# Two engine assignments for the splitting of weights in the first MoE: odd lo parts on VectorE, every third low word on ScalarE

## The chip, the cores and the metric

The kernel runs on one core of one Trainium2 chip. The time is device microseconds of one execution. Three runs of the kernel before took 1201.35 to 1202.64 us, with a median of 1201.83.

## The reference, cut to what matters

Attention over 4 batches of 12 heads (448 tokens, 64 per head, with RMS norm of q and k) is followed by two MoE blocks without a gate. All weights arrive as float64.

```python
scores = scale * q_n @ k_n.T
attn = exp(scores - max) / sum
x = (attn @ v).transpose(0, 2, 1, 3).reshape(1792, 768)
h = x @ w_in                    # 768 x 2048
x2 = (relu(h) ** 2) @ w_out     # 2048 x 768
y = ((x2 @ w1) * (x2 @ w2)) @ w3 @ moe2_w_out
```

## The kernel before, in words

**Three products for one.** TensorE multiplies float32 operands as fp32r, with fewer bits. So each operand is kept as two parts: hi, the value copied into fp32r, and lo, the value less hi. `mm3` (its matmuls are lines 403, 404 and 405) adds up hi x hi, hi x lo and lo x hi. A part of a weight is a stationary 128x128 block, the activations of one batch (448 tokens) move.

**From float64 to two parts.** A weight unit is a block of 128 x 384 or 128 x 512 weights. On its first use it comes from HBM as pairs of 32-bit words, into one of four `raw64` buffers (`load_next`, the DMA on line 313, SyncE's queue). `words` makes the high word into the top bits of a float32 on ScalarE (line 327) and the low word's top 16 bits into its lowest bits, either on ScalarE (line 331) or on GpSimd (line 333); which of them is read from `LOW_ENG`. `join` shifts and ors the two on VectorE (line 340) into a float32 tile in a `raw` buffer, and so frees the `raw64` buffer. `store` writes that tile to a scratch tensor (`f_in`, `f_out`, `f_1`, `f_2`) on SyncE's queue (line 348), from where later batches load it as float32. `split_hi` copies it into the hi part on ScalarE (line 138, by `copy_on`). `split_lo` subtracts hi from it into the lo part, on VectorE or GpSimd (line 145, by `sub_on`); which of them is read from `LO_ENG`. The lo part is the last reader of the `raw` buffer.

**Units.** `units` lists them in order of use. Numbers 0 to 31 belong to the product w3 x w_out of the second MoE, which is made first. Numbers 32 to 119 are the float64 units of the first batch's MoE: 32 of w_in (384 wide), 24 of w_out (512 wide), 32 of w1 and w2 (384 wide), in the order 16 of w_in, 12 of w_out, 16 of w_in, 12 of w_out, 32 of w1 and w2. All later ones are float32. `U0` is 32 and `U1` is 120, so `LOW_ENG[1]` and `LO_ENG[1]` are read for 32 to 119 alone; from 120 on the lo part has a rule of its own.

**Order of the work.** The loop over 48 heads at the end of the kernel mixes each head's attention with a generator of matmuls (`fill`): w3 x w_out beside batch 0's heads, the first batch's MoE (`gen_moe(0)`) beside batch 1's heads, and so on. `advance(u)` keeps the loads five units, the words three, the joins two and the hi parts one unit ahead of the lo parts, and the lo parts four ahead of the unit in use. The order in which an engine issues is not the emitted one: a planner of the framework chooses it from its own costs of the instructions. Only from the third batch on SyncE's queue is held to the emitted order, and every engine in the tail (`in_order`, `chain`).

**Attention on the same engines.** For a head, TensorE makes scores `sc` (lines 925 and 926), VectorE their maxima `nb` (927), ScalarE the exponents `p` (949), TensorE turns them into `pt` (985), ScalarE copies that into the hi part of `ptr` (138), VectorE makes its lo part (145) and TensorE multiplies by v into `kv` (1026). In the second batch p goes through a DMA `pw<-p` on the way (955). `ql` (897) is a part of the next head's q on VectorE; `act` is the activation inside the MoE (474 to 479), whose lo part is on VectorE for the first batch; `x` is the attention's output, whose lo part is on GpSimd.

The two tables of engines, and the lines that read them:

```python
LOW_ENG = ("gga", "g")                 # 65
LO_ENG = ("ggggv", "ggv")              # 66
low_eng = LOW_ENG[i >= U0]             # words, 329
if low_eng[i % len(low_eng)] == "a":   # 330
lo_eng = LO_ENG[i >= U0]               # split_lo, 368
eng = lo_eng[i % len(lo_eng)] if i < U1 else "g"
```

Of the kernel before, what the change touches and what calls it, by code (L numbers as in the profile page):

```python
# [30 lines left out]
def attention_moe_kernel(  # L31
# [30 lines left out]

    LOW_ENG = ("gga", "g")
    LO_ENG = ("ggggv", "ggv")
    KHI_ENG = "ggvv"
    KLO_ENG = "gvvv"
    QHI_ENG = "avvv"
# [254 lines left out]
    def words(i):  # L324
# [3 lines left out]
        low = t.rearrange("p n t -> p (n t)").bitcast(U16).rearrange("p (n t) -> p n t", t=4)[:, :n, 1]  # L328
        low_eng = LOW_ENG[i >= U0]
        if low_eng[i % len(low_eng)] == "a":  # L330
# [34 lines left out]
    def split_lo(i):  # L365
        n = units[i][0].shape[-1]
        t = hls[i]
        lo_eng = LO_ENG[i >= U0]
        if i >= u_at["pair"]:
# [837 lines left out]
```

## Time and profile before

| | us |
|---|---|
| median of three runs | 1201.83 (1201.35 to 1202.64) |
| the profiled execution | 1196.79 |
| its span, first to last instruction | 1195.0 |
| share of TensorE's full clock, mean over the span | 0.978 |

The profile is of one execution. PE is TensorE's matrix unit, PEld its weight load, DVE is VectorE, ACT is ScalarE, POOL is GpSimd, SPq is SyncE's queue of DMAs. A row of the table by stretch has the stretch, its length, then for PE, PEld, DVE, ACT and POOL the busy us with the number of instructions, the granted clock as a share of full speed, the DMA engines' share and GB/s. A row of a group has the line, the engine, the operation, out<-in by the program's names, shapes and count; then the busy us and the mean ns of one; then the engine's idle time just before the group's instructions and what ended it. A row of waits has who waited for whom, the us in total, how often and the longest. A row of one line has the shortest, the middle and the longest duration in ns. A row of the timeline has the start in us, the duration in us, the instruction, and in brackets its engine's idle time before it with what ended that. A matmul's duration overlaps with the next one's.

### The profile page before, as it was taken

To read this page: it belongs to the slowest core of one execution; us is meant where nothing else is said; L and a number is where in the kernel's file an instruction comes from. 1 tells how busy PE (TensorE), PEld (TensorE's weight loads), DVE (VectorE), ACT (ScalarE), POOL (GpSimd) and SP (SyncE) were. 2 spreads that over 40 slices of the span, in tenths; PEclk is the share of its full clock that TensorE was granted. 3 is DMA by queue.
4 is the path that set the end of the run, shared out by engine and by line. 5 is a ranking of instruction groups with operands and counts; after the bars stand their busy time and mean duration, and the time that the engine had idled before them with its cause. 6 is when DMAs were issued, how large, how long until landed. Compare 5 with 4: busy or idle time off the path is not lost.

```text
span 1195.0 us, 19065 instructions
## 1 busy us (share of the span) xinstructions
PE 1148.4 (96%) x6054; PEld 1033.2 (86%) x6054; DVE 783.7 (66%) x1311; ACT 781.8 (65%) x1802; POOL 721.7 (60%) x708
## 2 busy tenths in 40 slices
PE   7799999998998999999999999999999999999998
PEld 4588788887897879998989999998999999799997
DVE  6689888877877854665565565564543213887786
ACT  6799878767767766767766677676773535433352
POOL 6776535555676766766785767485774858421131
PEclk8699999999998999999999999999999999999999
DMA  7777757788877884566664657665555656343433
GB/s 233 225 222 214 224 152 224 263 260 270 261 262 256 271 257 150 173 176 185 185 204 145 197 168 246 194 204 155 176 156 178 186 167 187 96 130 108 124 89 118
DMA packets 127811, 229.74 MB, mean 192 GB/s; under 512 B 15744, under 2 KB 80480, under 8 KB 127712
## 3 DMA queue, kind: packets, MB, share of 16 engines
q1 hardware_dynamic: 125984, 225.79, 61.9%
q10 hardware_dynamic: 1728, 2.75, 0.6%
q8 instruction: 47, 0.77, 0.3%
q14 instruction: 52, 0.43, 0.1%
HBM read 162.53 MB, written 37.05 MB: 167 GB/s over the span
## 4 chain that ended last, share of the span: by engine, by line
PE 53%; DMA 4%; ACT 4%; DVE 3%; issue 2%; POOL 2%; SPq 0%; ACTq 0%; POOLq 0%; DVEq 0%
PE mm L403 13%; PE mm L404 13%; PE mm L405 13%; PE kv L1026 3%; PE pt L985 2%; DMA raw<-w 1%; PE sc L926 1%; PE sc L925 1%; ACT p L949 1%; PE pt L404 1%; PE pt L405 1%; PE sc L404 1%; PE sc L405 1%; PE sc L403 1%; PE pt L403 1%
## 5 line engine op out<-in xcount | busy, mean ns | idle before, releaser
L145 POOL TENSOR_TENSOR hl<-raw,hl 128x384 fp32r<-128x384 f32 (+1 forms) x317 | 379.3, 1204 | 228.6 <-ACT hl L138 180.1
L138 ACT ACTIVATE hl<-raw 128x384 fp32r<-128x384 f32 (+1 forms) x405 | 226.5, 565 | 158.0 <-PE mm L405 32.4
L404 PE MATMUL mm<-x,hl 128*128 128x448 f32 (+1 forms) x640 | 237.5, 371 | 7.9 <-POOL x L145 7.9
L403 PE MATMUL mm<-x,hl 128*128 128x448 f32 (+1 forms) x640 | 240.5, 376 | 0.6 <-ACT x L138 0.6
L405 PE MATMUL mm<-x,hl 128*128 128x448 f32 (+1 forms) x640 | 236.3, 369 | 0.0
L404 PE MATMUL mm<-act,hl 128*128 128x448 f32 (+1 forms) x544 | 200.9, 369 | 5.1 <-POOL act L145 3.6
L403 PE MATMUL mm<-act,hl 128*128 128x448 f32 (+1 forms) x544 | 203.3, 374 | 0.8 <-ACT act L477 0.8
L405 PE MATMUL mm<-act,hl 128*128 128x448 f32 (+1 forms) x544 | 199.3, 367 | 0.0
L927 DVE TENSOR_REDUCE nb<-sc 112x1 f32<-112x448 f32 x192 | 115.3, 617 | 86.9 <-PE sc L926 85.7
L949 ACT ACTIVATE p<-sc,nb,rr 112x448 f32<-112x448 f32 x192 | 138.2, 722 | 5.8 <-DVE nb L929 3.4
L404 PEld LDWEIGHTS mm<-x,hl 128*128 128x128 f32 x640 | 122.9, 192 | 19.0 <-POOL x L145 9.8
L403 PEld LDWEIGHTS mm<-x,hl 128*128 128x128 f32 x640 | 122.8, 192 | 10.5 <-ACT x L138 1.0
L405 PEld LDWEIGHTS mm<-x,hl 128*128 128x128 f32 x640 | 123.0, 192 | 9.8
L333 POOL TENSOR_SCALAR raw<-raw 128x384 uint32<-128x384 uint16 (+1 forms) x110 | 77.4, 704 | 76.4 <-DMA raw<-w_in 31.5
L340 DVE SCALAR_TENSOR_TENSOR raw<-raw 128x384 uint32<-128x384 uint32 (+1 forms) x120 | 95.1, 800 | 43.3 <-POOL raw L333 24.5
L145 DVE TENSOR_TENSOR ptr<-pt,ptr 128x448 fp32r<-128x448 f32 x144 | 86.2, 617 | 52.4 <-ACT ptr L138 52.2
L404 PEld LDWEIGHTS mm<-act,hl 128*128 128x128 f32 x544 | 103.5, 190 | 15.5 <-POOL act L145 6.3
L403 PEld LDWEIGHTS mm<-act,hl 128*128 128x128 f32 x544 | 103.8, 191 | 8.8 <-ACT act L477 1.2
L405 PEld LDWEIGHTS mm<-act,hl 128*128 128x128 f32 x544 | 103.6, 190 | 7.8
L478 DVE TENSOR_TENSOR gf<-mm,r 128x448 f32<-128x448 f32 x64 | 39.6, 620 | 80.6 <-ACT r L474 76.0
L327 ACT ACTIVATE raw<-raw 128x384 f32<-128x384 f32 (+1 forms) x120 | 70.4, 595 | 29.2 <-DMA raw<-w_in 14.5
L145 POOL TENSOR_TENSOR act<-gf,act 128x448 fp32r<-128x448 f32 x64 | 77.0, 1204 | 13.3 <-DMA pw<-p 4.9
(149 smaller groups left out, 2188.7 us busy)
## 6 DMA issues: line engine op xcount, KB each, us to landing
pw<-p SPq DMA_DIRECT2D x72, 392.0 KB
raw<-f_in SPq DMA_DIRECT2D x96, 192.0 KB
raw<-f_out SPq DMA_DIRECT2D x72, 256.0 KB
raw<-w_in SPq DMA_DIRECT2D x32, 384.0 KB
raw<-w_out SPq DMA_DIRECT2D x24, 512.0 KB
raw<-w SPq DMA_DIRECT2D x32, 384.0 KB
qt<-q_t SPq DMA_DIRECT2D x48, 224.0 KB
raw<-f SPq DMA_DIRECT2D x56, 192.0 KB
```

Source lines behind the costliest of these rows:

```text
L138: nc.scalar.activation(out=out, in_=in_, func=AF.Copy)
L145: (nc.vector if eng == "v" else nc.gpsimd).tensor_tensor(out=out, in0=in0, in1=in1, op=op)
L327: nc.scalar.activation(out=hi, in_=hi, func=AF.Prelu, scale=2.0**-112, alpha=-(2.0**32))
L333: nc.gpsimd.tensor_scalar(out=t[:, :n, 0], in0=low, scalar1=2.0**-13, scalar2=2.0**-14 - 0.5, op0=ALU.mult, op1=ALU.add)
L340: nc.vector.scalar_tensor_tensor(out=f[:, :n].bitcast(U32), in0=t[:, :n, 1], scalar=3, in1=t[:, :n, 0], op0=ALU.logical_shift_left, op1=AL ...
L403: nc.tensor.matmul(ps, w[:, 0, wk, :], x[0], start=(i == 0), stop=False)
L404: nc.tensor.matmul(ps, w[:, 0, wk, :], x[1], start=False, stop=False)
L405: nc.tensor.matmul(ps, w[:, 1, wk, :], x[0], start=False, stop=(i == last))
L478: nc.vector.tensor_tensor(out=gf, in0=ps, in1=r, op=ALU.mult)
L927: nc.vector.tensor_reduce(out=nb[:, j:j + 1], in_=o[j], axis=AX.X, op=ALU.max, negate=True)
L949: nc.scalar.activation(out=p, in_=o[j], func=AF.Exp, scale=d["rq"][:, c:c + 1], bias=nb[:, j:j + 1], accum_out=sm[:, i, c:c + 1],)
L1026: nc.tensor.matmul(ps[:, :S], w, m, start=(n == 0), stop=(n == len(ops) - 1))
```

## The change

```diff
-    LOW_ENG = ("gga", "g")
-    LO_ENG = ("ggggv", "ggv")
+    LOW_ENG = ("gga", "gga")
+    LO_ENG = ("ggggv", "gv")
```

Of units 32 to 119, those whose number leaves 2 when divided by 3 (30 units: 22 of 384 and 8 of 512) have their low word made on ScalarE, where all 88 were on GpSimd. The lo part is made on VectorE for the odd numbers (44 units: 32 of 384 and 12 of 512), where it was for those that leave 2 when divided by 3 (30 units: 22 and 8); the others are on GpSimd. What is computed, the buffers and the transfers stay.

## Rows read from the trace of the kernel before

**Rows 1.** The page, part 1: busy us, share of the span, instructions.

```profile
PE 1148.4 (96%) x6054; PEld 1033.2 (86%) x6054; DVE 783.7 (66%) x1311; ACT 781.8 (65%) x1802; POOL 721.7 (60%) x708
```

**Rows 2.** The table by stretch, for the first MoE and what follows.

```profile
99.00:434.00 335.00, 313.24 (x1698) 279.32 (x1697) 276.36 (x474) 255.08 (x611) 201.71 (x219) 0.98 0.77 242
...
434.00:1195.00 761.00, 752.24 (x3955) 688.82 (x3953) 435.64 (x703) 449.85 (x1026) 451.73 (x410) 0.99 0.55 166
```

**Rows 3.** Waits of PE, 99 to 434 us.

```profile
PE sc L925 <- ACT p L949: 6.4, 10, 1.8
PE pt L985 <- DVE ptr L145: 6.2, 7, 2.7
PE pt L985 <- DMA pw<-p: 3.3, 2, 2.2
PE mm L404 <- DVE act L145: 1.5, 1, 1.5
PE kv L1026 <- DVE ptr L145: 1.4, 1, 1.4
PE mm L404 <- POOL x L145: 1.3, 2, 0.8
```

**Rows 4.** The table by stretch, of a piece at half clock.

```profile
361.40:368.10 6.70, 6.08 (x21) 5.18 (x22) 6.21 (x13) 3.65 (x11) 5.28 (x7) 0.50 0.99 347
```

**Rows 5.** Groups of POOL by shape, 99 to 434 us: low words and lo parts.

```profile
L145 POOL TENSOR_TENSOR hl<-raw,hl 128x384 fp32r<-128x384 f32 x42 | 48.1, 1148 | 17.1 <-ACT hl L138 14.9 <-PE kv L1026 0.8
L333 POOL TENSOR_SCALAR raw<-raw 128x384 uint32<-128x384 uint16 x64 | 41.0, 640 | 53.5 <-DMA raw<-w_in 31.5 <-DMA raw<-w 11.5 <-DVE vhl L142 4.0
L145 POOL TENSOR_TENSOR hl<-raw,hl 128x512 fp32r<-128x512 f32 x22 | 31.5, 1435 | 6.2 <-ACT hl L138 5.5
L333 POOL TENSOR_SCALAR raw<-raw 128x512 uint32<-128x512 uint16 x24 | 20.3, 846 | 15.9 <-DMA raw<-w_out 10.9 <-DVE nb L927 1.7 <-PE sc L926 1.4
```

**Rows 6.** Groups of ACT by shape, 0 to 120 us: low words.

```profile
L331 ACT ACTIVATE raw<-raw 128x512 uint32<-128x512 uint16 x5 | 3.4, 671 | 0.0
...
L331 ACT ACTIVATE raw<-raw 128x384 uint32<-128x384 uint16 x5 | 2.8, 550 | 0.0
```

**Rows 7.** Timeline of ACT, two evictions and the next one.

```profile
145.84 0.96 ACT L138 ACTIVATE ptr<-pt 128x448 fp32r<-128x448 f32 x2
146.69 0.54 ACT L138 ACTIVATE kt<-kv 128x448 fp32r<-128x448 f32 x1
```

**Rows 8.** Groups of DVE by shape, 99 to 434 us: joins and lo parts.

```profile
L340 DVE SCALAR_TENSOR_TENSOR raw<-raw 128x384 uint32<-128x384 uint32 x64 | 49.6, 783 | 32.2 <-POOL raw L333 15.7 <-ACT raw L327 6.3 <-POOL hl L145 4.3
...
L340 DVE SCALAR_TENSOR_TENSOR raw<-raw 128x512 uint32<-128x512 uint32 x27 | 24.8, 929 | 3.8 <-POOL raw L333 3.0 <-DMA raw<-w_out 0.5 <-issue 0.3
L145 DVE TENSOR_TENSOR hl<-raw,hl 128x384 fp32r<-128x384 f32 x22 | 15.6, 708 | 1.8 <-ACT hl L138 1.7
...
L145 DVE TENSOR_TENSOR hl<-raw,hl 128x512 fp32r<-128x512 f32 x9 | 7.4, 819 | 0.0
```

**Rows 9.** Line 340 on DVE, 99 to 434 us: durations, idle before it.

```profile
L340 DVE SCALAR_TENSOR_TENSOR raw<-raw x91: 543/678/2369, 101.8 to 426.5; 128x384 uint32<-128x384 uint32 x64, 128x512 uint32<-128x512 uint32 x27
...
  POOL raw L333: 18.7, 12
  ACT raw L327: 6.3, 4
  POOL hl L145: 4.3, 4
```

**Rows 10.** Line 145 on DVE, 99 to 434 us: durations of weights' lo parts.

```profile
L145 DVE TENSOR_TENSOR hl<-raw,hl x31: 543/675/1374, 123.9 to 432.9; 128x384 fp32r<-128x384 f32 x22, 128x512 fp32r<-128x512 f32 x9
```

**Rows 11.** Timeline around 320 us: POOL, DVE and the matmul behind them.

```profile
319.93 1.29 POOL L145 TENSOR_TENSOR hl<-raw,hl 128x512 fp32r<-128x512 f32 x1 [0.95 <-ACT hl L138]
...
320.54 1.17 DVE L897 SCALAR_TENSOR_TENSOR ql<-qt,gg,qh 128x448 fp32r<-128x448 f32 x1
...
322.30 0.47 PE L404 MATMUL mm<-act,hl 128*128 128x448 f32 x1 [1.47 <-DVE act L145]
```

## The prediction

> **What bounds the kernel now.** The page comes first. It says that TensorE's matrix unit was busy 1148.4 of 1195.0 us, 96%, while VectorE, ScalarE and GpSimd stood at 66%, 65% and 60% [rows 1]: only TensorE's 46.6 idle us, and what it lost at half clock, can be won back by moving work between the other three. The second view is the table by stretch, for the change touches 88 weight units that are handled between 99 and 434 us and nothing else. In that stretch TensorE is busy 313.2 of 335.0 us, so it is idle 21.8 us, and its mean granted clock is 0.98 [rows 2]. Behind 434 us it is idle only 761.0 - 752.2 = 8.8 us: what is gained or lost in the stretch is handed to the end almost whole, and nothing behind it can be gained by this change.
>
> The same table gives the three helpers there: VectorE 276.4 us (82%), ScalarE 255.1 (76%), GpSimd 201.7 (60%) [rows 2]. The change takes work from the idlest and gives it to the two busiest.
>
> The third view is who TensorE waited for in that stretch [rows 3]. The reader should see two things. No matmul waits for a weight (hl): every row is attention or activation work. And by engine the waits are ScalarE 6.4 us (the exponents p), VectorE 6.2 + 1.5 + 1.4 = 9.1, a DMA 3.3, GpSimd 1.3. GpSimd, which the change relieves, is directly behind 1.3 us of 21.8. The weights matter only through the queues: an instruction of theirs stands in front of an exponent or of a part of p.
>
> The clock belongs to the price of a stall. Of the stretch's time 2% of full clock is missing, that is 0.02 x 335 / 0.5 = 13.4 us at the lower level, 1.2 GHz. One such piece, 361.4 to 368.1, is at 0.50 [rows 4]; the engine was busy 6.08 of its 6.7 us, and work done there takes twice as long, so it cost some 3.4 us, and one of half its length would cost 1.7. All that could come back in the stretch is thus 21.8 + 6.7 = 28.5 us.
>
> **The change part by part.** The units are numbered 32 to 119: 64 of 128x384 words and 24 of 128x512.
>
> *Low words.* Every third unit (number mod 3 = 2) is 22 narrow and 8 wide ones. GpSimd loses 22 x 0.640 + 8 x 0.846 = 20.8 us [rows 5]. ScalarE gets the same ones in the form it already runs on the first 32 units: 22 x 0.550 + 8 x 0.671 = 17.5 us [rows 6]. Neighbours on ScalarE overlap: two evictions take 0.96 us together, and the next one starts at 146.69, before they end at 146.80 [rows 7]. Less 0.11 us each, the queue grows by 17.5 - 3.3 = 14.2 us, and ScalarE's idle time falls from 79.9 to 65.7 us.
>
> *Lo parts.* Before, 30 units (mod 3 = 2) go to VectorE; after, the 44 odd ones. 29 move to VectorE and 15 move back, so the net is 14: 10 narrow, 4 wide. GpSimd loses 10 x 1.148 + 4 x 1.435 = 17.2 us [rows 5]; VectorE gains 10 x 0.708 + 4 x 0.819 = 10.4 us [rows 8]. GpSimd goes to 201.7 - 20.8 - 17.2 = 163.7 us, 49% of the stretch.
>
> *What VectorE gets back.* Its instructions that read two operands from SBUF are stretched. The narrow join takes 0.783 us on average and 0.543 at best, the narrow lo part 0.708 and 0.543 [rows 8 to 10]. That is 64 x 0.240 + 22 x 0.165 = 19.0 us; the wide joins at the same share of their 24.8 us add 7.6. With 38.0 / 201.7 = 19% less GpSimd work I take 19% of 26.6 us: 5.0 us. The bounds are nothing, if the pairs that meet stay the same, and all 26.6.
>
> How GpSimd stretches VectorE is to be seen at 320 us: a GpSimd lo part runs from 319.93 to 321.22, VectorE's ql starts at 320.54 inside it and takes 1.17 us, and a matmul that needs the next result stands 1.47 us [rows 11]. The Trainium skill (SBUF — State Buffer, section on the two separate sides) has GpSimd and a VectorE instruction with two SBUF inputs exclude each other for a whole instruction. By that rule ql, which alone would take 0.543 x 448 / 384 = 0.63 us by the narrow join's rate (an estimate), would end near 321.85; it ended at 321.71, so the row shows a hold somewhat shorter than the rule's. By the rule a join would lose half a GpSimd instruction of some 1 us in 60% of cases before and 49% after, 0.055 us less on each of 91 joins and some 31 lo parts: 6.6 us as an estimate, against 5.0 by rows; the sum would fall by 0.5 us.
>
> *Waits of the join.* VectorE stands behind GpSimd's low word 15.7 + 3.0 = 18.7 us [rows 8], behind ScalarE's high word 6.3 and behind GpSimd's lo part (which frees the buffer that the join writes) 4.3 [rows 9]. What is queued behind a join is all that VectorE does: maxima, parts of p, activations. With 30 of 88 low words gone from GpSimd, 18.7 falls by 6.4, and 4.3 by a fifth, 0.8. What is late next in these 30 is ScalarE, which makes high and low word one after the other: 0.55 us more where the join stood for its words. 12 + 4 of 91 joins did [rows 9]; 30 x 0.55 x 16/91 = 2.9 us comes back, or 16.5 if all 30 are late.
>
> *Transfers.* No DMA is added, removed or moved to another queue. GpSimd's low words waited 31.5 + 11.5 + 10.9 = 53.9 us for the loads themselves [rows 5]; a faster GpSimd doesn't make these land sooner, save where the join that frees a load's buffer comes sooner. I cost this at nothing; without that cover (a join later than now) SyncE's queue is held, and with it the copies of p that 3.3 us of waits are for [rows 3].
>
> **The sum.** TensorE's waits are scaled by the room left on the engine behind them. VectorE: +10.4 - 5.0 - 6.4 - 0.8 + 2.9 = +1.1 us; its room is 335.0 - 276.4 - 29.3 (the waits above) = 29.3 us, and 9.1 x 29.3 / 28.2 - 9.1 = +0.4 us. ScalarE: 6.4 x 79.9 / 65.7 - 6.4 = +1.4 us if the waits for p come from its queue, nothing if they come from what it waited for; its longest is no row of a busy queue, so I take the middle, +0.7. GpSimd: 1.3 x 163.7 / 201.7 - 1.3 = -0.3. Together +0.8 us. Bounds: ScalarE's 14.2 us whole on the path, +14; VectorE's 9.1 and the half-clock 6.7 both gone, -16. On the profiled execution, 1196.8 us (a span of 1195.0 and 1.8 around it), this makes 1197.6; the three runs have a median of 1201.83, 5.0 more, and on them it is 1202.6. A measurement here can tell some 0.2%, 2.4 us, from no change, so the likeliest case is that nothing is seen, with a range of its own of 1199.4 to 1204.2.
>
> **The rivals.**
> *A, VectorE is freed: faster.* VectorE is busy or held behind words 276.4 + 29.3 = 305.7 of 335.0 us [rows 2, 8]; it is the engine nearest to its limit and stands behind the most waits. If the relief comes out nearer to its upper bound, half of the 9.1 us goes, and one half-clock piece 3.4 us long with it: -4.5 - 1.7 = -6.2, 1195.6 us. For it: the stall of [rows 11], which comes straight from the overlap with GpSimd. Against it: VectorE also gets 10.4 us of work. Chance 0.25.
> *B, ScalarE becomes late: slower.* Exponents, evictions of p and both weight parts share its queue. TensorE waits for p ten times now [rows 3]; if a low word lands ahead of an exponent or eviction that TensorE needs in 9 of 30 cases, that is 9 x 0.55 = 5.0 us, and one more half-clock piece, 1.7: +6.7, 1208.5. It decides once waits for ScalarE exceed some 9 us instead of 6.4. For it: 76% goes to 80%. Against it: 20% stays free. Chance 0.21.
> *C, the planner orders the stretch anew.* The order on each engine up to there isn't written out; a planner makes it from costs of its own, and other engines give another order. A stall like the longest of [rows 3], 2.7 us, with a piece like that of [rows 4], 3.4 us, may go or come: 1195.7 or 1207.9, each at 0.09.
> That the change doesn't reach its units can be left out: both indices are the unit's number, and all 88 pass them.
>
> **How the numbers follow.** No visible change 0.36; faster 0.25 + 0.09 = 0.34; slower 0.21 + 0.09 = 0.30. The range reaches to the cases on both sides and a little further for the unknown bounds: 1194.5 to 1210.
>
> **What would show it.** In the stretch: GpSimd near 164 us, ScalarE near 269 to 273, VectorE 281 to 287; joins nearer to 0.72 than 0.78 us; VectorE's wait for GpSimd's low words near 12 us and a new one for ScalarE's. If waits for p grow to 9 us and more, B holds; if waits for VectorE's parts of p halve, A does. A span that moves over 5 us while these busy times come out as said would make the scaling by room wrong; a move behind 434 us would make the first part wrong.

## The result, and the profile after

The changed kernel takes 1181.82 us (median of six runs, 1179.11 to 1189.06), the one before 1199.82 (six runs, 1194.99 to 1202.64). The ratio is 0.9873, with an interval of 0.985 to 0.9896: faster by 1.3%. The forecast was no visible change, 1202.6 us, in a range from 1194.5 to 1210.

Part 1 of the page of the changed kernel, with the span:

```profile
span 1177.9 us, 19026 instructions
...
PE 1133.2 (96%) x6054; PEld 1021.6 (87%) x6054; DVE 781.3 (66%) x1325; ACT 794.7 (67%) x1832; POOL 683.3 (58%) x664
```

Against [rows 1] GpSimd lost 38.4 us, VectorE lost 2.4 and ScalarE gained 12.9. TensorE's own busy time fell by 15.2 us with the same 6054 matmuls. Its mean granted clock over the span rose from 0.978 to 0.991; what is missing to full clock fell from 0.022 x 1195.0 = 26.3 to 0.009 x 1177.9 = 10.6 us, 15.7 less, which accounts for these 15.2.

To compare equal work, the stretch is ended in each kernel by the same event, the first matmul of the 23rd head's product with v. That is at 443.8 us before and at 426.3 after. The table by stretch, of the kernel before with this end, and what follows:

```profile
99.00:443.80 344.80, 323.04 (x1740) 288.31 (x1739) 283.07 (x484) 261.09 (x625) 210.36 (x225) 0.98 0.77 243
443.80:1195.00 751.20, 742.44 (x3912) 679.84 (x3911) 428.94 (x692) 443.84 (x1011) 443.08 (x403) 0.99 0.55 164
```

The same of the changed kernel:

```profile
99.00:426.30 327.30, 314.05 (x1746) 282.66 (x1745) 286.21 (x499) 275.74 (x659) 171.92 (x182) 1.00 0.80 255
426.30:1177.90 751.60, 739.41 (x3912) 677.26 (x3910) 425.56 (x692) 443.23 (x1010) 443.60 (x404) 1.00 0.55 165
```

The stretch is 344.8 - 327.3 = 17.5 us shorter, what follows as long as before (751.2 and 751.6). TensorE's idle time in it falls from 21.8 to 13.2 us, 8.6 less, and its clock rises from 0.98 to 1.00. The kernel before ran four pieces of the stretch at half clock, one of them that of [rows 4]:

```profile
129.30:132.60 3.30, 3.30 (x14) 3.19 (x13) 3.02 (x6) 3.16 (x9) 2.26 (x3) 0.50 0.98 333
282.90:286.20 3.30, 3.30 (x10) 2.94 (x9) 3.03 (x5) 3.04 (x9) 1.15 (x3) 0.50 1.02 368
...
433.10:436.40 3.30, 3.30 (x11) 2.95 (x10) 3.30 (x6) 3.18 (x8) 2.98 (x2) 0.50 0.93 314
```

Together they are 16.6 us long; at half clock that costs some 8.3 us, an estimate from these rows. The changed kernel has no such piece in its stretch. Less idle time and the full clock make 16.9 of the 17.5 us. The helpers moved as the forecast had it: GpSimd -38.4 (forecast -38.0), ScalarE +14.7 (+14.2), VectorE +3.1 (+5.4).

Who TensorE waited for in the stretch of the changed kernel (us in total, times, longest):

```profile
PE sc L925 <- ACT p L949: 6.0, 8, 1.2
PE pt L985 <- DVE ptr L145: 3.9, 5, 1.0
PE pt L985 <- DMA pw<-p: 1.7, 3, 0.7
PE mm L403 <- ACT r L138: 0.5, 1, 0.5
PE mm L404 <- POOL x L145: 0.3, 1, 0.3
```

Against [rows 3], the waits for p are nearly the same (6.0 us instead of 6.4), the ones for VectorE went from 9.1 to 3.9 us, and the longest is 1.2 us instead of 2.7. The list of before is the same when its stretch is taken to 443.8, save for one more wait of 0.8 us for ScalarE.

The joins and lo parts on VectorE, the same stretch:

```profile
L340 DVE SCALAR_TENSOR_TENSOR raw<-raw 128x384 uint32<-128x384 uint32 x64 | 46.3, 731 | 16.2 <-POOL raw L333 9.8 <-ACT raw L331 4.3 <-POOL hl L145 0.9
...
L340 DVE SCALAR_TENSOR_TENSOR raw<-raw 128x512 uint32<-128x512 uint32 x27 | 21.5, 805 | 1.5 <-POOL raw L333 1.1 <-issue 0.4
L145 DVE TENSOR_TENSOR hl<-raw,hl 128x384 fp32r<-128x384 f32 x32 | 20.7, 648 | 1.7 <-ACT hl L138 1.6
...
L145 DVE TENSOR_TENSOR hl<-raw,hl 128x512 fp32r<-128x512 f32 x13 | 13.1, 1004 | 0.0
```

Line 340's idle time by what ended it:

```profile
  POOL raw L333: 10.9, 11
  ACT raw L331: 4.3, 5
  POOL hl L145: 0.9, 1
```

Against [rows 8, 9] VectorE stands 16.2 + 1.5 = 17.7 us in front of joins instead of 32.2 + 3.8 = 36.0. GpSimd's low word holds it 10.9 us instead of 18.7, its lo part 0.9 instead of 4.3; the high word of ScalarE, 6.3 before, is gone from the list, and the low word of ScalarE holds it 4.3.

The lo parts and low words on GpSimd and ScalarE's new ones:

```profile
L145 POOL TENSOR_TENSOR hl<-raw,hl 128x384 fp32r<-128x384 f32 x32 | 35.6, 1114 | 32.3 <-ACT hl L138 28.9 <-DMA raw<-w_out 2.5
L145 POOL TENSOR_TENSOR hl<-raw,hl 128x512 fp32r<-128x512 f32 x22 | 30.7, 1402 | 14.3 <-ACT hl L138 11.4 <-issue 1.6 <-DMA f_out<-raw 0.9
L333 POOL TENSOR_SCALAR raw<-raw 128x384 uint32<-128x384 uint16 x42 | 27.8, 661 | 39.2 <-DMA raw<-w_in 16.5 <-DMA raw<-w 10.7 <-issue 6.0
...
L333 POOL TENSOR_SCALAR raw<-raw 128x512 uint32<-128x512 uint16 x16 | 14.1, 884 | 23.4 <-DMA raw<-w_out 12.6 <-DVE act L145 4.4 <-DVE raw L340 4.3
```

```profile
L331 ACT ACTIVATE raw<-raw 128x384 uint32<-128x384 uint16 x22 | 12.2, 553 | 0.0
...
L331 ACT ACTIVATE raw<-raw 128x512 uint32<-128x512 uint16 x8 | 5.4, 681 | 0.0
```

The 30 low words have the forecast's prices on ScalarE, 553 and 681 ns. The lo parts on VectorE cost 648 and 1004 ns, where the forecast had 708 and 819.

### The profile page after: what moved, and what is told of

It reads as the page before. It is cut to its first block, busy times and chain, and to the rows that moved or that the text cites. A ratio compares the mean times of both kernels' runs of the same rounds, so it can differ in the third digit from the quotient of the medians.

```text
span 1177.9 us, 19026 instructions
## 1 busy us (share of the span) xinstructions
PE 1133.2 (96%) x6054; PEld 1021.6 (87%) x6054; DVE 781.3 (66%) x1325; ACT 794.7 (67%) x1832; POOL 683.3 (58%) x664
## 4 chain that ended last, share of the span: by engine, by line
PE 45%; ACT 13%; DMA 13%; DVE 9%; issue 4%; POOL 2%; SPq 2%; ACTq 0%; DVEq 0%; POOLq 0%
PE mm L403 11%; PE mm L404 11%; PE mm L405 10%; ACT p L949 3%; ACT hl L138 2%; PE kv L1026 2%; PE pt L985 2%; DMA raw<-w_out 2%; DMA raw<-f_in 2%; DMA pw<-p 2%; DMA raw<-w 1%; DMA raw<-w_in 1%; ACT raw L327 1%; DMA raw<-f 1%; DMA raw<-f_out 1%
## 5 line engine op out<-in xcount | busy, mean ns | idle before, releaser
L145 POOL TENSOR_TENSOR hl<-raw,hl 128x384 fp32r<-128x384 f32 (+1 forms) x303 | 360.1, 1196 | 255.0 <-ACT hl L138 211.7
L404 PE MATMUL mm<-x,hl 128*128 128x448 f32 (+1 forms) x640 | 234.4, 366 | 6.9 <-POOL x L145 6.7
L403 PE MATMUL mm<-x,hl 128*128 128x448 f32 (+1 forms) x640 | 237.5, 371 | 0.6 <-ACT r L138 0.5
L405 PE MATMUL mm<-x,hl 128*128 128x448 f32 (+1 forms) x640 | 233.0, 364 | 0.0
L404 PEld LDWEIGHTS mm<-x,hl 128*128 128x128 f32 x640 | 120.9, 189 | 17.5 <-POOL x L145 8.8
L403 PEld LDWEIGHTS mm<-x,hl 128*128 128x128 f32 x640 | 120.7, 189 | 10.4 <-ACT r L138 0.8
L405 PEld LDWEIGHTS mm<-x,hl 128*128 128x128 f32 x640 | 120.8, 189 | 9.3
L340 DVE SCALAR_TENSOR_TENSOR raw<-raw 128x384 uint32<-128x384 uint32 (+1 forms) x120 | 88.8, 748 | 26.3 <-POOL raw L333 18.7
L333 POOL TENSOR_SCALAR raw<-raw 128x384 uint32<-128x384 uint16 (+1 forms) x80 | 58.4, 730 | 70.9 <-DMA raw<-w_in 16.5
L327 ACT ACTIVATE raw<-raw 128x384 f32<-128x384 f32 (+1 forms) x120 | 70.7, 598 | 23.7 <-DMA raw<-w 10.1
```

Of the source, the lines that this page charges most:

```text
L145: (nc.vector if eng == "v" else nc.gpsimd).tensor_tensor(out=out, in0=in0, in1=in1, op=op)
L327: nc.scalar.activation(out=hi, in_=hi, func=AF.Prelu, scale=2.0**-112, alpha=-(2.0**32))
L333: nc.gpsimd.tensor_scalar(out=t[:, :n, 0], in0=low, scalar1=2.0**-13, scalar2=2.0**-14 - 0.5, op0=ALU.mult, op1=ALU.add)
L340: nc.vector.scalar_tensor_tensor(out=f[:, :n].bitcast(U32), in0=t[:, :n, 1], scalar=3, in1=t[:, :n, 0], op0=ALU.logical_shift_left, op1=AL ...
L403: nc.tensor.matmul(ps, w[:, 0, wk, :], x[0], start=(i == 0), stop=False)
L404: nc.tensor.matmul(ps, w[:, 0, wk, :], x[1], start=False, stop=False)
```

## The experiments

The ratios are to the kernel before, with their 95% intervals. "The stretch" ends as above, with the same matmul. Each kernel has one profile, of one of its executions. The edits are against the kernel before or the changed one, as the text says; where they write to `spare`, a tile of that name which nobody reads is added too.

**The halves.** First the low words alone.

```diff
-    LOW_ENG = ("gga", "g")
+    LOW_ENG = ("gga", "gga")
```

> The 30 low words go to ScalarE, the lo parts stay as before (every third on VectorE). Theory J (joins stood behind GpSimd's low words, and with them VectorE's parts of p; the low words are the cause): most of the gain of 1.3%, a ratio of 0.988 to 0.992, the join's idle time near 20 us instead of 36. Theory L (the lo parts are the cause: they clear GpSimd's queue): 0.996 to 1.002, as ScalarE's 17 us more are not paid for. Theory O (the planner's new order is the cause, not the load): anything from 0.985 to 1.01, without relation to the join's waits.

Ratio 0.9911 (0.9889 to 0.9932). Then the lo parts alone.

```diff
-    LO_ENG = ("ggggv", "ggv")
+    LO_ENG = ("ggggv", "gv")
```

> The lo parts of odd units go to VectorE, all low words stay on GpSimd. Theory J: little, 0.996 to 1.003, the join's idle time over 28 us, since 88 low words still come from GpSimd and VectorE has 10 us more. Theory L: most of the gain, 0.988 to 0.992. Theory O: anything from 0.985 to 1.01.

Ratio 0.9952 (0.9933 to 0.9971). Both halves bring a part, 0.9% and 0.5%, together about what the whole change brings. Neither J nor L holds alone: J's ratio for the low words came out, its idle time of the joins did not. The joins of the run with the low words alone:

```profile
L340 DVE SCALAR_TENSOR_TENSOR raw<-raw 128x384 uint32<-128x384 uint32 x64 | 46.0, 727 | 30.4 <-POOL raw L333 13.0 <-ACT raw L331 8.5 <-POOL hl L145 3.2
...
L340 DVE SCALAR_TENSOR_TENSOR raw<-raw 128x512 uint32<-128x512 uint32 x27 | 22.7, 849 | 3.9 <-POOL raw L333 2.5 <-ACT raw L331 1.0 <-issue 0.4
```

and with the lo parts alone:

```profile
L340 DVE SCALAR_TENSOR_TENSOR raw<-raw 128x384 uint32<-128x384 uint32 x64 | 46.1, 727 | 27.2 <-POOL raw L333 13.7 <-ACT raw L327 6.1 <-POOL hl L145 4.4
...
L340 DVE SCALAR_TENSOR_TENSOR raw<-raw 128x512 uint32<-128x512 uint32 x27 | 22.7, 850 | 2.9 <-POOL raw L333 2.1 <-ACT raw L327 0.5 <-issue 0.3
```

Alone, the low words leave the joins' idle time as it was (34.3 us; GpSimd's part fell to 15.5, ScalarE's low word took 9.5 of it over), and what they gained goes with shorter joins, 0.727 us instead of 0.783: VectorE is busy 277.8 us instead of 283.1. The lo parts alone bring it to 30.1. Only both together bring it to 17.7. Both profiles are of the longest of four executions, 1193.71 us where the median is 1188.76, and 1194.72 where it is 1193.12, so their idle times may be somewhat high.

**Load or order.** The same loads on other units, for the kernel after and for the one before.

```diff
-    LOW_ENG = ("gga", "gga")
-    LO_ENG = ("ggggv", "gv")
+    LOW_ENG = ("gga", "gag")
+    LO_ENG = ("ggggv", "vg")
```

> The same loads as in the changed kernel, other units: the low words of those that leave 1 when divided by 3 (29 instead of 30) on ScalarE, the lo parts of the even units on VectorE. Theories J and L: as fast as the changed kernel within 0.4%, a ratio of 0.983 to 0.992, no piece at half clock between 100 and 420 us or one at most. Theory O: the gain is that of one order, so this one differs from it by over 0.5%, 0.993 to 1.005 being likelier than 0.987.

```diff
-    LO_ENG = ("ggggv", "ggv")
+    LO_ENG = ("ggggv", "gvg")
```

> The loads of the kernel before, other units: the lo parts of units that leave 1 when divided by 3 (29 instead of 30) on VectorE. Theories J and L: within 0.4% of the kernel before. Theory O: off by 0.5% and more, either way.

0.9864 (0.984 to 0.9887), like the changed kernel, and 1.0016 (0.9995 to 1.0037), like the one before. Theory O falls as far as one other assignment for each load can show it: the load counts, not the one order that the planner made. The run with the changed kernel's loads had two pieces at half clock (178.7 to 182.0 and 332.3 to 335.6), where one at most was expected.

**More of ScalarE.** Half of the low words there.

```diff
-    LOW_ENG = ("gga", "gga")
+    LOW_ENG = ("gga", "ga")
```

> The changed kernel, but every second low word of units 32 to 119 on ScalarE (44 instead of 30: GpSimd some 9 us less, ScalarE 8 us more). If GpSimd's low words are still what the joins wait for, a further gain of 0.2 to 0.5% on the changed kernel, a ratio of 0.982 to 0.985. If ScalarE, at 85% of the stretch, is next, no gain or a loss: 0.987 to 0.995, with more waits for p.

Ratio 0.9835 (0.9805 to 0.9865). The joins' idle time falls to 11.4 us, but VectorE is 4.4 us busier and the profiled stretch is as long as the changed kernel's. The two intervals overlap (0.9865 above, 0.985 below), so a further gain is not shown. The next run puts ScalarE's 17 us into the kernel before, with nothing taken from GpSimd.

```diff
+        if i >= U0 and i % 3 == 2:
+            nc.scalar.activation(out=spare[:, :n], in_=hi, func=AF.Copy)
```

> The kernel before with 30 more ScalarE copies right behind the high words of every third unit (a result that nobody reads), some 17 us: what ScalarE pays for the change, without what GpSimd gets. If ScalarE is near the path (rival B's price): 1.003 to 1.006. If ScalarE's room takes it: 0.998 to 1.002.

Ratio 0.9971 (0.995 to 0.9992). ScalarE's row in the table by stretch has it at 276.0 us, as in the changed kernel, and the time does not rise:

```profile
99.00:442.10 343.10, 322.21 (x1744) 288.50 (x1743) 284.72 (x485) 276.00 (x658) 209.02 (x227) 0.98 0.77 244
```

Rival B falls by this. That the run is a little faster than the kernel before has no cause that was tried.

**What GpSimd's work costs.** The changed kernel with 35 us of work put back on GpSimd.

```diff
+        if U0 <= i < U1 and i % 3 == 2:
+            hi = t[:, 0, :n].bitcast(F32)
+            nc.gpsimd.tensor_tensor(out=spare[:, :n], in0=hi, in1=hi, op=ALU.subtract)
```

> The changed kernel with 30 more GpSimd subtractions of a unit's hi part (a result that nobody reads), 34 to 38 us, so that GpSimd is as busy as before, while ScalarE and VectorE keep what the change gave them. Theory Q (what counts is how long GpSimd's queue is, whatever is in it): the gain goes, a ratio of 0.996 to 1.004, the join's idle time over 28 us. Theory H (what counts is that 30 joins no longer need an answer from GpSimd at all): most of the gain stays, 0.987 to 0.992.

And with memsets in place of the subtractions.

```diff
+        if U0 <= i < U1 and n == 384:
+            for _ in range(2):
+                nc.gpsimd.memset(t[:, 1, 384:].bitcast(F32), 0.0)
```

> The changed kernel with 128 GpSimd memsets of columns that nobody reads, two per narrow unit: GpSimd is busy again, but reads nothing from SBUF. Theory Q by occupation alone: as the run with 30 more subtractions, in proportion to the us added. If what counts is that GpSimd's two-operand instructions stretch VectorE's: the gain stays, 0.986 to 0.990, and the joins stay near 0.73 us. Theory H: the gain stays too.

0.9926 (0.9902 to 0.9951) and 0.9866 (0.9834 to 0.9898). The added group and the stretch of the run with subtractions:

```profile
L380 POOL TENSOR_TENSOR spare<-hl 128x384 bf16<-128x384 f32 x22 | 24.8, 1125 | 6.8 <-ACT hl L139 6.3 <-PE pt L992 0.4
...
L380 POOL TENSOR_TENSOR spare<-hl 128x512 bf16<-128x512 f32 x8 | 10.0, 1251 | 4.5 <-DMA f_out<-raw 4.4
```

```profile
99.00:437.20 338.20, 320.63 (x1746) 286.46 (x1745) 297.24 (x499) 275.06 (x657) 205.76 (x212) 0.98 0.78 246
```

and of the run with memsets:

```profile
L376 POOL MEMSET hl<- 128x128 f32 x126 | 26.2, 211 | 16.8 <-PE mm L408 12.2
```

```profile
99.00:426.40 327.40, 314.56 (x1735) 284.02 (x1734) 281.43 (x497) 274.06 (x655) 197.15 (x307) 0.99 0.80 254
```

Both bring GpSimd to 197 to 206 us, near the 210 of before. With subtractions VectorE is busy 297.2 us instead of 286.2 and the stretch is 10.9 us longer; with memsets VectorE is at 281.4 and the stretch as long as in the changed kernel. The subtractions take back some 0.5 of the 1.3%, which is between what theories Q and H wanted, and the joins' idle time is 19.6 us, not over 28. Theory Q (a long queue) falls by the memsets. The Trainium skill (SBUF — State Buffer, section on the two separate sides) has a VectorE instruction with two SBUF inputs exclude only GpSimd instructions that read SBUF; these two rows agree.

Three more runs changed what GpSimd does there. Short subtractions:

```diff
+        if U0 <= i < U1 and n == 384:
+            hi = t[:, 0, :128].bitcast(F32)
+            nc.gpsimd.tensor_tensor(out=spare[:, :128], in0=hi, in1=hi, op=ALU.subtract)
```

> The changed kernel with 64 short GpSimd subtractions of 128 columns of a hi part, one per narrow unit (a result that nobody reads), 25 to 30 us: as many us as the 126 memsets, in short instructions like them, but reading from SBUF. Theory K (GpSimd's reads stretch VectorE's two-operand instructions, and VectorE's time is the path): VectorE some 6 to 9 us busier than in the changed kernel, a ratio of 0.991 to 0.996. Theory S (the long subtractions of the run with 30 more cost because a low word stood behind each): as with the memsets, 0.985 to 0.989.

The long ones in two halves (the edit is against the run that put them back):

```diff
-            nc.gpsimd.tensor_tensor(out=spare[:, :n], in0=hi, in1=hi, op=ALU.subtract)
+            for h in (slice(0, n // 2), slice(n // 2, n)):
+                nc.gpsimd.tensor_tensor(out=spare[:, h], in0=hi[:, h], in1=hi[:, h], op=ALU.subtract)
```

> The changed kernel with the same 30 GpSimd subtractions as in the run that put them back, each in two halves. If the length of a GpSimd instruction is what holds VectorE and the low words behind it: VectorE some 3 to 6 us busier than in the changed kernel instead of 11, a ratio of 0.986 to 0.990. If it is the reads: as with whole ones, 0.990 to 0.995, VectorE 10 us busier or more.

One operand, against the same run:

```diff
-            nc.gpsimd.tensor_tensor(out=spare[:, :n], in0=hi, in1=hi, op=ALU.subtract)
+            for _ in range(2):
+                nc.gpsimd.tensor_scalar(out=spare[:, :n], in0=hi, scalar1=1.0, scalar2=1.0, op0=ALU.mult, op1=ALU.mult)
```

> The changed kernel with 60 GpSimd multiplications of one operand of a hi part (two per third unit, a result that nobody reads), 30 to 40 us: long reads of one operand. If a GpSimd instruction with two operands is what stretches VectorE's: as with the memsets, 0.986 to 0.990, VectorE at 280 to 288 us. If any long GpSimd instruction that reads does: 0.990 to 0.995, VectorE over 292 us.

The ratios are 0.9917 (0.9886 to 0.9947), 0.9923 (0.9889 to 0.9957) and 0.9897 (0.985 to 0.9944). Their stretches, in this order, and the group of the short ones:

```profile
99.00:427.70 328.70, 314.55 (x1744) 282.94 (x1743) 287.71 (x499) 275.58 (x659) 213.46 (x246) 1.00 0.80 254
```

```profile
99.00:433.80 334.80, 317.21 (x1738) 284.13 (x1738) 292.48 (x497) 274.25 (x655) 217.74 (x241) 0.99 0.79 248
```

```profile
99.00:433.10 334.10, 319.36 (x1737) 286.34 (x1736) 289.19 (x497) 273.65 (x655) 216.14 (x242) 0.98 0.79 250
```

```profile
L377 POOL TENSOR_TENSOR spare<-hl 128x128 bf16<-128x128 f32 x64 | 45.6, 712 | 21.9 <-ACT hl L139 10.4 <-DMA raw<-w_in 6.2 <-ACT nt L824 2.2
```

GpSimd is 42 to 46 us busier than in the changed kernel in all three, VectorE 1.5, 6.3 and 3.0 us. So it isn't the reads alone: VectorE paid 11.0 us for the whole subtractions (1.13 and 1.25 us each), 6.3 for the halves (0.79 and 1.02 us) and 1.5 for the short ones (0.71 us). The instructions with one operand, at 3.0, are shorter too (0.72 and 0.92 us), so these runs don't separate length from the number of operands. The order rests on one profile each, and kernels with the same loads differ by up to 3.3 us of VectorE's time (283.1, 282.2 and 279.8 with the loads of before, 286.2 and 285.2 with those of after), so 1.5 and 3.0 can't be told from nothing. No expectation of the three came out whole: the ratios of the first two are those of the reads, but VectorE's time is not, and the third lies between its two theories. The short ones took 45.6 us instead of 25 to 30; their stretch is only 1.4 us longer, and the rest of their loss lies behind it (1186.2 - 427.7 = 758.5 us against 751.6), for which nothing was tried.

What one pair costs can be read from the traces. Two pairs of the kernel before, then one of the run with memsets:

```profile
300.94 0.79 POOL L333 TENSOR_SCALAR raw<-raw 128x512 uint32<-128x512 uint16 x1 [1.39 <-PE sc L926]
...
301.24 0.90 DVE L145 TENSOR_TENSOR hl<-raw,hl 128x384 fp32r<-128x384 f32 x1
...
301.81 1.21 POOL L145 TENSOR_TENSOR hl<-raw,hl 128x384 fp32r<-128x384 f32 x1
...
302.19 1.39 DVE L340 SCALAR_TENSOR_TENSOR raw<-raw 128x512 uint32<-128x512 uint32 x1
```

```profile
333.87 0.21 POOL L376 MEMSET hl<- 128x128 f32 x1
333.88 0.55 DVE L340 SCALAR_TENSOR_TENSOR raw<-raw 128x384 uint32<-128x384 uint32 x1
```

VectorE's lo part ends 0.41 us after GpSimd's low word, which reads one operand, and the join 0.56 us after GpSimd's subtraction; beside the memset a join takes 0.55 us. The other pairs of the kernel before are alike. Of 40 joins and lo parts of 384 columns on VectorE that start in no GpSimd instruction 39 take 0.54 to 0.57 us; all nine that start inside a GpSimd subtraction of 384 columns end 0.41 to 0.43 us after it, and take up to 1.38 us. GpSimd is held too: its low word of 384 columns mostly takes 0.54 us, and 0.73 where it starts inside such a join or lo part. So a read of one operand holds VectorE as well, the hold ends with GpSimd's instruction, and part of the price lands on GpSimd. In the run with 30 more subtractions VectorE wasn't held by five of ten such pairs; there GpSimd's subtraction was the longer one, 1.25 to 1.84 us where the shortest took 0.82.

**What VectorE's work costs.** The changed kernel with 22 more subtractions there.

```diff
+        if U0 <= i < U1 and i % 4 == 2:
+            hi = t[:, 0, :n].bitcast(F32)
+            nc.vector.tensor_tensor(out=spare[:, :n], in0=hi, in1=hi, op=ALU.subtract)
```

> The changed kernel with 22 more VectorE subtractions of a hi part (a result that nobody reads), some 13 us. Theory K: VectorE's us are what the stretch pays in, so most of the 13 us come back, a ratio of 0.994 to 0.999. If it is the joins' waits for other engines that count, and VectorE's own time is hidden: 0.986 to 0.990.

Ratio 0.9997 (0.9971 to 1.0023): the whole gain is gone. The added group and the stretch:

```profile
L377 DVE TENSOR_TENSOR spare<-hl 128x384 bf16<-128x384 f32 x16 | 14.4, 898 | 0.2 <-ACT hl L139 0.2
...
L377 DVE TENSOR_TENSOR spare<-hl 128x512 bf16<-128x512 f32 x6 | 5.6, 942 | 0.0
```

```profile
99.00:441.80 342.80, 321.11 (x1750) 286.63 (x1749) 297.99 (x521) 276.83 (x663) 182.73 (x183) 0.99 0.78 245
```

VectorE is 11.8 us busier, its joins' idle time goes from 17.7 to 21.1, and the stretch is 15.5 us longer: these 11.8 + 3.4 = 15.2 us of VectorE are paid one to one. Less VectorE work, by the hi part of q on ScalarE:

```diff
-    QHI_ENG = "avvv"
+    QHI_ENG = "aavv"
```

> The changed kernel with the hi part of q in the second batch's heads (12 of 128x448) on ScalarE instead of VectorE: VectorE some 7 us less, ScalarE 8 us more, at 88% of the stretch. Theory K: faster than the changed kernel by 3 to 7 us, a ratio of 0.981 to 0.985. If ScalarE is the bound by now: 0.987 to 0.992.

Ratio 0.9869 (0.9837 to 0.9902), no gain, where theory K wanted 3 to 7 us: VectorE is 4.1 us less busy and stands 3.5 us longer in front of joins. So busy time taken off VectorE need not come back; whether ScalarE was in the way here is open. And all lo parts on VectorE:

```diff
-    LO_ENG = ("ggggv", "gv")
+    LO_ENG = ("ggggv", "v")
```

> The changed kernel with all lo parts of units 32 to 119 on VectorE: 44 more there (some 27 us at their unstretched 0.55 and 0.68 us), GpSimd 54 us less. Theory K: VectorE pays 27 us and gets back some 16 (34.8 us of GpSimd's subtractions cost it 11), so it is 10 us busier and the kernel slower than the changed one by 5 to 10 us, 0.991 to 0.996. If GpSimd's queue is what counts: a further gain, 0.980 to 0.985.

Ratio 0.9824 (0.9799 to 0.9849), against theory K: VectorE's busy time rises by 5.7 us only instead of 10, its joins' idle time falls to 14.6, and the stretch is 4.3 us shorter still.

```profile
99.00:422.00 323.00, 311.77 (x1746) 283.12 (x1745) 291.88 (x543) 277.27 (x661) 120.36 (x137) 1.00 0.81 257
```

**The sum that goes with the stretch.** VectorE's busy time plus its idle time in front of joins, from the table by stretch and the join's two groups of each profile:

| kernel | stretch, us | busy | before joins | sum | stretch less sum | ratio |
|---|---|---|---|---|---|---|
| before, other units (e4) | 348.0 | 282.2 | 40.6 | 322.8 | 25.2 | 1.0016 |
| words earlier (e16) | 345.4 | 279.8 | 41.1 | 320.9 | 24.5 | 0.9997 |
| before | 344.8 | 283.1 | 36.0 | 319.1 | 25.7 | 1 |
| ScalarE load (e9) | 343.1 | 284.7 | 28.3 | 313.0 | 30.1 | 0.9971 |
| VectorE load (e10) | 342.8 | 298.0 | 21.1 | 319.1 | 23.7 | 0.9997 |
| lo parts alone (e2) | 340.1 | 286.3 | 30.1 | 316.4 | 23.7 | 0.9952 |
| GpSimd put back (e7) | 338.2 | 297.2 | 19.6 | 316.8 | 21.4 | 0.9926 |
| low words alone (e1) | 337.2 | 277.8 | 34.3 | 312.1 | 25.1 | 0.9911 |
| halves (e14) | 334.8 | 292.5 | 22.0 | 314.5 | 20.3 | 0.9923 |
| one operand (e15) | 334.1 | 289.2 | 22.0 | 311.2 | 22.9 | 0.9897 |
| after, other units (e3) | 331.0 | 285.2 | 22.4 | 307.6 | 23.4 | 0.9864 |
| short reads (e12) | 328.7 | 287.7 | 19.8 | 307.5 | 21.2 | 0.9917 |
| half of the low words (e5) | 327.8 | 290.6 | 11.4 | 302.0 | 25.8 | 0.9835 |
| memsets (e8) | 327.4 | 281.4 | 21.2 | 302.6 | 24.8 | 0.9866 |
| after | 327.3 | 286.2 | 17.7 | 303.9 | 23.4 | 0.9873 |
| hi part of q (e11) | 326.1 | 282.1 | 21.2 | 303.2 | 22.9 | 0.9869 |
| all lo parts (e6) | 323.0 | 291.9 | 14.6 | 306.5 | 16.5 | 0.9824 |
| both further (e13) | 320.6 | 286.0 | 12.2 | 298.2 | 22.4 | 0.9761 |

The sum spans 24.6 us and the stretch 27.4; in 16 of 18 profiles the difference lies between 20.3 and 25.8 us. That difference is VectorE's idle time in front of everything else, by the way it is made; what the table shows is that it hardly moves, not why. The sum goes with the stretch better than with the ratio, for what follows the stretch is 749.3 to 758.5 us long in these profiles. Neither busy time nor idle time alone goes with the stretch: 298.0 us of busy time stand beside 342.8, 291.9 beside 323.0. A test that moves no load, against the kernel before:

```diff
-            upto("word", i + WORD_AHEAD, lambda k: is64(k) and words(k))
+            upto("word", i + WORD_AHEAD + (i >= U0), lambda k: is64(k) and words(k))
```

> The kernel before with the words of units 32 to 119 emitted four units ahead of the lo parts instead of three, no load moved. Theory T: if the joins' idle time falls from 36 us to 20 to 28, the time falls by as much, a ratio of 0.988 to 0.996; if the planner leaves the idle time as it is, 0.998 to 1.002. If the idle time falls and the time does not, T is wrong.

Ratio 0.9997 (0.9967 to 1.0027). The planner's order left more idle time, 41.1 us, with less busy time, so it takes nothing from the theory and adds little to it. The version that it suggests, against the changed kernel:

```diff
-    LOW_ENG = ("gga", "gga")
-    LO_ENG = ("ggggv", "gv")
+    LOW_ENG = ("gga", "ga")
+    LO_ENG = ("ggggv", "v")
```

> Every second low word on ScalarE and all lo parts of units 32 to 119 on VectorE: GpSimd keeps 44 low words of the 88 and no lo part. Theory T (the stretch is as long as VectorE's busy time plus its idle time in front of joins, and some 24 us): the joins wait some 10 us, VectorE is at 292, so a little faster than the run with all lo parts or as fast, a ratio of 0.978 to 0.983. If ScalarE, at 88%, is the bound: 0.984 to 0.990.

Ratio 0.9761 (0.9714 to 0.9807), 1171.99 us: faster than both kernels, and a little below theory T's range, into which the interval reaches. T's sum of 292 + 10 us came out as 286.0 + 12.2. Its stretch and its joins:

```profile
99.00:419.60 320.60, 312.36 (x1741) 283.55 (x1740) 286.02 (x542) 282.44 (x671) 107.75 (x123) 0.99 0.81 258
```

```profile
L340 DVE SCALAR_TENSOR_TENSOR raw<-raw 128x384 uint32<-128x384 uint32 x64 | 37.6, 590 | 11.5 <-POOL raw L333 6.8 <-ACT raw L331 3.8 <-ACT raw L327 0.8
...
L340 DVE SCALAR_TENSOR_TENSOR raw<-raw 128x512 uint32<-128x512 uint32 x27 | 18.7, 694 | 0.7 <-POOL raw L333 0.5
```

GpSimd is at 108 us, the narrow join at 0.590 us (0.783 before), and VectorE no busier than in the changed kernel although it makes all 88 lo parts.

## Why the prediction was wrong

**Right:** the place (the time behind the stretch is the same), the engines' loads, the price of each moved low word, that the join's wait for GpSimd's low words would be near 12 us (10.9), and that ScalarE's room takes its 17 us. Rival B, priced at +6.7 us, has none of it: ScalarE's work alone cost nothing (e9), and the waits for p are 6.0 us, not 9. Rival C's other orders moved the time by 0.1 and 0.2% (e3, e4).

**Wrong, the term of the join's waits.** The forecast had 29.3 us and let 6.4 + 0.8 go and 2.9 come back: 4.3 us net. It measured 36.0 - 17.7 = 18.3. GpSimd's low words went about as forecast (to 10.9 us, forecast 12.3), and ScalarE's new low word brought back 4.3 instead of 2.9. But ScalarE's high word (6.3), which the step held fixed, is gone, GpSimd's lo parts (4.3, forecast 3.5) fell to 0.9, and of the 6.7 us of other waits that it left out 1.6 are left. With either half alone the idle time in front of joins stayed at 34.3 and 30.1 us; why it falls so far with both together isn't settled.

**Wrong, the scaling by room.** This step failed on its own. The forecast knew that VectorE had only 29.3 us of room, but scaled only TensorE's 9.1 us of waits for VectorE by it, and so turned +1.1 us of VectorE into +0.4 us of time. With the measured change of the sum put in, -15.2 us, the same scaling gives 9.1 x 29.3 / (29.3 + 15.2) - 9.1 = -3.1 us; the stretch lost 17.5. The run with 22 more subtractions shows one to one, for work that is added. The prediction's own sign for this came out: the span moved by 17.1 us while the busy times moved about as said. Rival A, which called VectorE the engine nearest to its limit, was right about the engine, and its sign came out too (the waits for VectorE's parts of p fell from 7.6 to 3.9 us), but it was priced at -6.2 us. Paid one to one, the 15.2 us give 1201.8 - 15.2 = 1186.6, within the measured runs.

**Wrong, the clock.** The likeliest case let no half-clock piece go, and all 16.6 us of them went, some 8.3 us of time. The forecast's lower bound of -16 us lay close to the result by 6.7 us for such pieces and 9.1 for TensorE's waits for VectorE, of which 5.2 went; the range stopped 9 us short of that bound. Why all the pieces went isn't settled. Fewer pieces aren't needed for a gain: the runs with one half each have a clock of 0.97 in the stretch, the kernel before 0.98, and both are faster.

**Of VectorE's relief** the forecast had 5.0 us. By its price of 10.4 us for the added work, 3.1 us more busy time leave 7.3, inside its bounds. The `ql` of [rows 11] ended 0.49 us after GpSimd's subtraction, and the narrow joins end 0.41 to 0.43 after theirs, where 0.54 is their whole time: VectorE is held to the end of GpSimd's instruction, and a part of its own time, some 0.12 us of the join's, runs beside it.

## What to carry to other kernels

Before costing a move between helpers, look at the instructions that wait for the moved work, the joins here. Add the idle time in front of them to the busy time of their engine: VectorE has 319.1 of 344.8 us then. Where that leaves little room, don't scale a few visible waits of TensorE by it. Here 15.2 us more of this sum cost 15.5 us, and 4.1 us less busy time brought nothing, as the waits grew by 3.5. Work that reads from SBUF can be worth taking off GpSimd even if it lands on VectorE itself: the 44 lo parts that were still on GpSimd made VectorE 5.7 us busier, and the time fell. An engine's busy share said little here: GpSimd at 60% was what to relieve, ScalarE at 76% what could take it.

## What was not expected of the hardware

A GpSimd memset of 128 columns took 0.211 us on average, and with 126 of them VectorE was no busier (281.4 us against 286.2); a GpSimd subtraction of 128 columns took 0.712 us, the shortest 0.388. The price that VectorE pays for GpSimd's work depends on its form: 34.8 us of long two-operand instructions made VectorE 11.0 us busier, 45.6 us of the same in short pieces 1.5. Each of these is from one profile.
